# x + alpha * fx on one core: other cut points for the loads, and a last load that belongs to x

## The chip, the core and the metric

The kernel runs on one core of one Trainium2 chip. The metric is the device time of one execution in microseconds (us); lower is better. A profiled execution also has a span, from the first to the last instruction that the profiler records; the device time is a little longer than the span.

## What is computed

The reference is one line:

```python
def reference(x, fx, alpha):
    return x + alpha * fx
```

x and fx are 512 x 32 x 640 in bf16, alpha is a single bf16 number. So 20.97 MB of x and 20.97 MB of fx are read from HBM, and 20.97 MB are written back. Each element takes one multiplication and one addition.

## The kernel before

Each tensor is laid out as 128 rows, one for each SBUF partition. A row holds 80 units of K = 1024 elements (2 KiB each), that is 160 KiB. The whole of x stays in SBUF as one tile, `x_t`, and the result is written over it. fx passes through two buffers of the tile `f_t` (tag "f", two buffers), each as wide as the widest piece.

The three lists at the top of the kernel say how rows are cut: `X` (five loads of x), `F` (eight pieces of fx) and `S` (three stores), in units. A load moves the same stretch of all 128 rows. A row's stretch is one packet, so a load is 128 packets, and each of the 16 DMA engines moves eight of them; the three stores have rows of 64, 64 and 32 KiB. In this text a load's "row" is such a packet.

The order is written out by hand in `PLAN`, and each engine runs its own instructions in this order. The letters mean: `x i` and `f j` are loads, `c j` computes piece j, `s i` is a store, and `a` fetches alpha and spreads it over the partitions by a 1 x 128 matmul. All transfers, loads and stores alike, are issued by SyncE (SP in the profile) in `transfer` (line 79), one after the other, into one DMA queue. A computation is two VectorE (DVE) instructions: the product in place in `f_t` (line 97), then the sum into `x_t` (line 100).

What orders the work is this. Piece j of fx goes to the buffer that piece j-2 had, so SP may issue `f j` only when the sum of piece j-2 is done. While SP waits for that, everything behind it in `PLAN` waits too. A load of x needs no buffer to come free. A computation needs its piece of fx and all loads of x that cover its stretch. A store needs the sums of its stretch, and one entry holds the first store back further:

```python
LATE = {("s", 0): ("f", 6)}
```

With it, SP issues store 0 only after load `f 6` has landed. In the kernel before, one more load, `f 7` (units 77 to 80, rows of 6144 bytes), follows `f 6` in the queue, so it is under way when store 0 is issued.

Of the kernel before, what the change touches and what calls it, by code (L numbers as in the profile page):

```python
# [1 line left out]

# [4 lines left out]

ACT = mybir.ActivationFunctionType
ALU = mybir.AluOpType
F32 = mybir.dt.float32  # L10
BF16 = mybir.dt.bfloat16

K = 1024
P = 128


X = [(0, 4), (4, 22), (22, 44), (44, 66), (66, 80)]
F = [(0, 11), (11, 22), (22, 33), (33, 44), (44, 55), (55, 66), (66, 77), (77, 80)]
S = [(0, 32), (32, 64), (64, 80)]
N = 80  # L20

PLAN = """
x 0
x 1
a
f 0
f 1
x 2
c 0
f 2  # L30
c 1
f 3
x 3
c 2
f 4
c 3
f 5
x 4
c 4
f 6  # L40
c 5
f 7
c 6
s 0
s 1
c 7
s 2
"""
LATE = {("s", 0): ("f", 6)}


@with_exitstack
def kernel(
    ctx: ExitStack,
    tc: tile.TileContext,
    x: bass.AP,
    fx: bass.AP,
    alpha: bass.AP,
    out: bass.AP,
):  # L60
    nc = tc.nc
    xv = x.flatten_outer_dims().rearrange("(p n) d -> p (n d)", p=P)
    fxv = fx.flatten_outer_dims().rearrange("(p n) d -> p (n d)", p=P)
    ov = out.flatten_outer_dims().rearrange("(p n) d -> p (n d)", p=P)
    assert xv.shape[1] == N * K

    consts = ctx.enter_context(tc.tile_pool(name="consts", bufs=1))
    psum = ctx.enter_context(tc.tile_pool(name="psum", bufs=1, space=bass.MemoryType.PSUM))
    whole = ctx.enter_context(tc.tile_pool(name="whole", bufs=1))
    fs = ctx.enter_context(tc.tile_pool(name="fs", bufs=2))  # L70
    ctx.enter_context(tc.manual_schedule())

    sync = mybir.DependencyInfo(mybir.DependencyClass.Sync, mybir.DependencyReason.DATA)
    xt = whole.tile([P, N * K], x.dtype, name="x_t")
    ft, moved = {}, {}
    done = []

    def transfer(what, out, in_):
        r = nc.sync.dma_start(out=out, in_=in_)  # L79
        if what in LATE:  # L80
            tc.add_manual_dep(r.ins, moved[LATE[what]].ins.name, sync, reason="issue late")
        moved[what] = r
        done.append(r)

    def load_x(i):
        a, b = X[i]
        transfer(("x", i), xt[:, a * K : b * K], xv[:, a * K : b * K])

    def load_f(j):
        a, b = F[j]  # L90
        ft[j] = fs.tile([P, max(e - s for s, e in F) * K], fx.dtype, tag="f", name="f_t")
        transfer(("f", j), ft[j][:, : (b - a) * K], fxv[:, a * K : b * K])

    def compute(j):
        a, b = F[j]
        term, total = ft[j][:, : (b - a) * K], xt[:, a * K : b * K]
        nc.vector.tensor_scalar(  # L97
            out=term, in0=term, scalar1=lanes["a_f"][:], scalar2=None, op0=ALU.mult
        )
        done.append(nc.vector.tensor_tensor(out=total, in0=total, in1=term, op=ALU.add))  # L100

    def store(i):
        a, b = S[i]
        transfer(("s", i), ov[:, a * K : b * K], xt[:, a * K : b * K])

    lanes = {}

    def alpha_to_lanes():
        a_1 = consts.tile([1, 1], alpha.dtype, name="a_1")
        transfer("a", a_1[:], alpha[None, :])  # L110
        ones = consts.tile([1, P], alpha.dtype, name="ones")
        nc.vector.memset(ones[:], 1.0)  # L112
        a_ps = psum.tile([P, 1], F32, name="a_ps")
        done.append(nc.tensor.matmul(a_ps[:], ones[:], a_1[:], start=True, stop=True))  # L114
        lanes["a_f"] = consts.tile([P, 1], F32, name="a_f")
        nc.vector.tensor_copy(out=lanes["a_f"][:], in_=a_ps[:])  # L116

    does = {"x": load_x, "f": load_f, "c": compute, "s": store, "a": alpha_to_lanes}
    for step in PLAN.split("\n"):
        if step:  # L120
            what, *of = step.split()
            does[what](*map(int, of))

    rest = nc.sync.nop(nofuse=True)
    for i in done[:-1]:
        tc.add_manual_dep(rest.ins, i.ins.name, sync, reason="all but the last store")


# [1 line left out]
_INS = ['x', 'fx', 'alpha']  # L130
_OUTS = [((512, 32, 640), 'bfloat16')]


# [23 lines left out]
```

## Time and profile before

| what | value |
|---|---|
| median of 3 runs | 151.76 us (151.74 to 151.78) |
| the profiled execution's own time | 151.64 us |
| its span | 149.9 us |
| DVE busy | 67.0 us, 45% of the span, 18 instructions |
| PE, POOL busy | 0.2 us each |
| bytes moved by DMA | 62.92 MB in 2306 packets, one queue |
| time that the packets took | 97.9% of what 16 DMA engines have in the span |
| mean rate | 420 GB/s over the span |

The difference between the profiled execution's time and its span, 1.74 us, lies before the first and behind the last recorded instruction. The profiled execution is 0.12 us below the median of the runs.

The profile gives, for each DMA, the time of its issue on SP and the times at which its 16 shares landed (one for each DMA engine). The trace also has a record of each packet: its start, its duration and its size. It doesn't name the DMA engine of a packet.

### The profile page before, as it was taken

What the parts mean: (1) busy time and instruction counts of PE and PEld (TensorE: products, weight loads), DVE (VectorE), ACT (ScalarE), POOL (GpSimd) and SP (SyncE); (2) the same over time, 40 slices, a digit from 0 to 9 for tenths busy, and PEclk for the clock granted to TensorE, in tenths of its full rate; (3) what the DMA queues carried; (4) which work ended last, traced back from release to release, by engine and by line L of the source; (5) the groups of instructions that cost most, each with busy time, mean ns of one, the idle gap of its engine ahead of it and who ended that gap; (6) DMA issues with size and microseconds to landing.
All of it is one profiled execution on the core that took longest, in us unless ns stands there. A gap on an engine that the chain in (4) does not pass through costs nothing.

```text
span 149.9 us, 95 instructions
## 1 busy us (share of the span) xinstructions
PE 0.2 (0%) x1; PEld 0.1 (0%) x1; DVE 67.0 (45%) x18; POOL 0.2 (0%) x4
## 2 busy tenths in 40 slices
PE   0000000000000000000000000000000000000000
PEld 0000000000000000000000000000000000000000
DVE  0000008999900799991059999379940000000000
POOL 0000000000000000000000000000000000000000
DMA  5999899989989998898999999999796969989993
GB/s 171 473 423 472 385 439 427 481 385 505 457 349 421 433 529 385 385 481 385 433 433 423 452 421 430 409 490 525 315 542 297 560 280 560 455 385 394 429 420 157
DMA packets 2306, 62.92 MB, mean 420 GB/s; under 512 B 258, under 2 KB 258, under 8 KB 386
## 3 DMA queue, kind: packets, MB, share of 16 engines
q1 hardware_dynamic: 2306, 62.92, 97.9%
HBM read 41.94 MB, written 20.97 MB: 420 GB/s over the span
## 4 chain that ended last, share of the span: by engine, by line
DMA 46%; DVE 26%; SPq 1%; issue 0%; DVEq 0%
DMA f_t<-in_fx_dram 46%; DVE x_t L100 17%; DVE f_t L97 9%; SPq L79 1%; DVEq L97 0%
## 5 line engine op out<-in xcount | busy, mean ns | idle before, releaser
L100 DVE TENSOR_TENSOR x_t<-x_t,f_t 128x11264 bf16<-128x11264 bf16 (+1 forms) x8 | 43.9, 5492 | 0.3
L97 DVE TENSOR_SCALAR f_t<-f_t,a_f 128x11264 bf16<-128x11264 bf16 (+1 forms) x8 | 23.1, 2883 | 26.9 <-DMA f_t<-in_fx_dram 26.9
L116 DVE COPY a_f<-a_ps 128x1 f32<-128x1 f32 x1 | 0.2, 158 | 15.4 <-PE a_ps L114 15.4
L112 DVE MEMSET ones<- 1x128 bf16 x1 | 0.2, 165 | 0.8 <-PEq L141 0.8
L114 PE MATMUL a_ps<-a,ones 1*128 1x1 bf16 x1 | 0.2, 158 | 16.2 <-DMA a<-in_alpha_dram 16.2
L141 POOL MEMSET const-bfloat16-1.0<- 128x1 bf16 x1 | 0.1, 101 | 0.0
L141 POOL MEMSET const-uint8-127<- 128x1 uint8 x1 | 0.1, 101 | 0.0
L114 PEld LDWEIGHTS <-ones 1*128 1x128 bf16 x1 | 0.1, 100 | 1.0 <-DVE ones L112 1.0
L141 POOL MEMSET const-float32-0.0<- 128x1 f32 x1 | 0.1, 98 | 0.2 <-issue 0.2
L141 POOL MEMSET const-float32-1.0<- 128x1 f32 x1 | 0.1, 98 | 0.0
## 6 DMA issues: line engine op xcount, KB each, us to landing
f_t<-in_fx_dram SPq DMA_DIRECT2D x7, 2816.0 KB, 17.4
x_t<-in_x_dram SPq DMA_DIRECT2D x2, 5632.0 KB, 34.0
x_t<-in_x_dram SPq DMA_DIRECT2D x1, 4608.0 KB, 15.2
out_dram<-x_t SPq DMA_DIRECT2D x1, 4096.0 KB, 38.7
x_t<-in_x_dram SPq DMA_DIRECT2D x1, 3584.0 KB, 23.2
x_t<-in_x_dram SPq DMA_DIRECT2D x1, 1024.0 KB, 4.7
f_t<-in_fx_dram SPq DMA_DIRECT2D x1, 768.0 KB, 5.9
out_dram<-x_t SPq DMA_DIRECT2D x2, 31.1
```

The lines of the kernel that those rows point to most:

```text
L79: r = nc.sync.dma_start(out=out, in_=in_)
L97: nc.vector.tensor_scalar(out=term, in0=term, scalar1=lanes["a_f"][:], scalar2=None, op0=ALU.mult)
L100: done.append(nc.vector.tensor_tensor(out=total, in0=total, in1=term, op=ALU.add))
L112: nc.vector.memset(ones[:], 1.0)
L114: done.append(nc.tensor.matmul(a_ps[:], ones[:], a_1[:], start=True, stop=True))
L116: nc.vector.tensor_copy(out=lanes["a_f"][:], in_=a_ps[:])
L141: nc = _bacc.Bacc("TRN2", target_bir_lowering=False, num_devices=1)
```

## The change

K becomes 512, so that a unit is 1 KiB and a row has 160 of them; this alone moves no data differently. In KiB of a row, the cut points before and after are:

| | before | after |
|---|---|---|
| loads of x | 8, 36, 44, 44, 28 | 8, 38, 46, 23, 39, 6 |
| pieces of fx | 22 x 7, 6 | 23 x 6, 22 |
| stores | 64, 64, 32 | 64, 64, 32 |

The short load of 6 KiB rows, which was the last piece of fx (`f 7`), is now the last piece of x (`x 5`). It stands behind `f 6` in `PLAN` again, but its destination is a part of `x_t`, which no earlier work holds. With `f 7`, the computation `c 7` and its two DVE instructions are gone, and `c 6`, the last one now, also reads what `x 5` brings. `x 4` moves ahead of `c 3` and `f 5`. The two `f_t` buffers are 23 KiB a row where they were 22. The entry in `LATE` is the same. The bodies of the functions are not touched; their lines are one lower in number.

```diff
-K = 1024
+K = 512
 P = 128
...
-X = [(0, 4), (4, 22), (22, 44), (44, 66), (66, 80)]
-F = [(0, 11), (11, 22), (22, 33), (33, 44), (44, 55), (55, 66), (66, 77), (77, 80)]
-S = [(0, 32), (32, 64), (64, 80)]
-N = 80
+X = [(0, 8), (8, 46), (46, 92), (92, 115), (115, 154), (154, 160)]
+F = [(0, 23), (23, 46), (46, 69), (69, 92), (92, 115), (115, 138), (138, 160)]
+S = [(0, 64), (64, 128), (128, 160)]
+N = 160
...
 x 3
 c 2
 f 4
+x 4
 c 3
 f 5
-x 4
 c 4
 f 6
+x 5
 c 5
-f 7
 c 6
 s 0
 s 1
-c 7
 s 2
 """
 LATE = {("s", 0): ("f", 6)}
```

SP's order of issues is then x 0, x 1, a, f 0, f 1, x 2, f 2, f 3, x 3, f 4, x 4, f 5, f 6, x 5, s 0, s 1, s 2. Before it was x 0, x 1, a, f 0, f 1, x 2, f 2, f 3, x 3, f 4, f 5, x 4, f 6, f 7, s 0, s 1, s 2.

## The prediction

> **What bounds the kernel now.** I read the page's DMA lines first, then the queue's own waits, the timeline, the windows, and last the packet records. The page:
>
> ```profile
> span 149.9 us, 95 instructions
> PE 0.2 (0%) x1; PEld 0.1 (0%) x1; DVE 67.0 (45%) x18; POOL 0.2 (0%) x4
> q1 hardware_dynamic: 2306, 62.92, 97.9%
> DMA 46%; DVE 26%; SPq 1%; issue 0%; DVEq 0%
> ```
>
> The chain (last line) gives DVE 26%, but the 16 DMA engines are busy for 97.9% of the span: the chain follows instructions, and an instruction may wait while the queue stays full. Two windows, the loads and the stores (columns: stretch, us, busy of PE, PEld, DVE, POOL, clock, DMA share, GB/s):
>
> ```profile
> 1.70:97.50 95.80, 0.16 (x1) 0.00 (x0) 54.96 (x13) 0.00 (x0) 1.00 1.00 430
> 99.46:148.80 49.34, 0.00 (x0) 0.00 (x0) 10.87 (x4) 0.00 (x0) 1.00 0.99 427
> ```
>
> So the queue is full from the first packet (1.74 us) to the last (148.78 us). The end is set by bytes, rows, and what single engines lose. The timeline around the handover from loads to stores:
>
> ```profile
> 85.67 3.15 DVE L97 TENSOR_SCALAR f_t<-f_t,a_f 128x11264 bf16<-128x11264 bf16 x1
> 88.85 6.03 DVE L100 TENSOR_TENSOR x_t<-x_t,f_t 128x11264 bf16<-128x11264 bf16 x1
> 94.91 0.33 SPq L79 DMA_DIRECT2D f_t<-in_fx_dram  x1
> 98.45 0.82 SPq L79 DMA_DIRECT2D out_dram<-x_t  x2
> 98.46 3.15 DVE L97 TENSOR_SCALAR f_t<-f_t,a_f 128x11264 bf16<-128x11264 bf16 x1 [3.58 <-DMA f_t<-in_fx_dram]
> ```
>
> The short load f 7 is issued at 94.91, when the sum of c 5 frees its buffer, and its first row starts at 97.55: 2.64 us of notice, the least of any load but the first ones. Its rows of 6144 bytes take 236 ns at the median, but four of its 16 first rows took 638, 1287, 620 and 633 ns. No later row of it exceeds 245. Nothing like that is in the loads before it: all 896 rows of 22 KiB take 836 to 848 ns, first rows too. The one other place is the load with no notice, x 0 (issued at 0.73, first row at 1.74): rows of 309 ns whose 16 first ones take 354 to 892. The late engines stay late: the landings of the 16 shares spread over 0.44 us for f 6 (98.00 to 98.44), 0.87 for f 7 (99.93 to 100.80), 0.89 for the last store (148.22 to 149.11).
>
> **The change, part by part.**
>
> *Bytes and rows: nothing.* Rows of 22 and 44 KiB take 839 and 1665 ns at the median: 826 ns for 22 KiB, so 37.5 ns per KiB and 13 ns per row. This gives 238 for 6 KiB (measured 236) and 2416 for 64 KiB (2418). Before, the loads take 309 + 1364 + 7 x 839 + 2 x 1665 + 1065 + 236 = 12,177 ns per row set; after, x has 309 + 1440 + 1740 + 877 + 1477 + 236 and fx 6 x 877 + 839, together 12,180. Both have 13 loads. Eight rows per engine: +0.02 us. Stores are unchanged.
>
> *DVE: nothing on the path.* Seven pairs for eight. From 11264 and 3072 elements (6.03 and 1.76, 3.15 and 1.01 us) a pair costs 0.37 us at length zero, which is saved under the stores; a pair of 23 KiB takes 9.53 us from start to start, where one of 22 KiB takes 9.13 (23.15 to 32.28). The last sum ends at 110.4 both before (108.64 + 1.76) and after; store 2 is needed only when store 1's rows run out, at 138.1. Its cover is 27 us.
>
> *Does the queue run dry?* I add up the landings: f 0 lands at 23.05 + 0.60 + 0.30 = 23.95; each 23 KiB load then takes 7.01 us, 46 KiB 13.93, 39 KiB 11.82, 22 KiB 6.71. Landings: f 1 30.97, x 2 44.9, f 2 51.9, f 3 58.9, x 3 65.9, f 4 72.9, x 4 84.7, f 5 91.7, f 6 98.45, x 5 about 100.4. DVE: c 0 from 24.05, c 1 to 43.2, c 2 from 51.95 to 61.55, c 3 to 71.1, c 4 to 82.55, c 5 from 91.8 to 101.4, c 6 to 110.4. So the issues on SP: f 2 33.7, f 3 43.2, x 3 43.6, f 4 61.55, x 4 61.9, f 5 71.1, f 6 82.55, x 5 82.9. The tightest is f 4: its first row is due at 65.0 (x 3's landing less 0.9, by f 6 and f 7: 98.44 and 97.55), 3.45 us after its issue; a row follows its issue by 1.01 us (x 0), so 2.4 us are spare. Moving x 4 ahead of f 5 on SP makes it 6.6 us earlier than 68.55 and delays nobody: f 5 waits for c 3 anyway. x 5 waits for no buffer.
>
> *The handover.* Store 0 is issued when f 6 lands, 98.45, as before, with 6144-byte rows under way, as before; its first row started at 99.47 with no gap behind the front engine. Store 1 now waits for c 5's sum (101.4; before, f 7 had waited for it), with SP's queue holding only store 2 behind it; its rows are needed at 118.8. Cost nothing, cover 17 us.
>
> *The slow first rows.* This is where the change can act: x 5 is issued about 82.9, some 14.6 us ahead of its first row. If the slow rows come from the short notice, they go. What they cost: by order of time the hit engines are the first to finish f 6 (+1.05), the second or so, the eleventh and the last (+0.4 each). The third and fourth latest of the final landings are 148.68 and 148.60; the latest is 149.11. Taking the three late ones away leaves 148.60, a gain of 0.51; by the completion packets (148.78 down to 148.18) it is 0.59. If only the 1287 ns row went, 149.11 less 148.89, 0.22. Nothing would be late next: the queue only shifts. I take 0.5, near the landings. At the other bound they all stay (0), or they hit worse (below).
>
> The Trainium skill speaks against this part. Its page "DMA: Bandwidth & Descriptors", section "Latency and other measured facts", gives about 0.6 us from an HWDGE issue to the first byte; f 7's notice is four times that, so by the page the early issue gains nothing and the sum would be 151.76. The trace shows 1.01 us (x 0), also less than 2.64, yet four engines were slow; so the row alone does not settle it.
>
> **Rivals.**
>
> 1. *The notice was short (forecast).* For: only f 7 among the later loads has less than 3 us, and only it and x 0 have slow first rows; the next shortest, f 6 (issued 85.78, started 90.8, 5 us), has none. The times of three runs lie within 0.04 us, so this is no chance event of one run. Against: 12 of 16 engines were not slow with the same notice. Time: 151.76 + 0.02 - 0.5 = 151.28; with some of f 4's first rows slow, up to 151.45. In the profiled execution: span 149.4, time 151.16.
>
> 2. *The slow first rows belong to the short rows behind long ones.* For: f 7 is also the only load of 6144-byte rows; less than 0.25 us of work per row covers less of a read's delay. Against: rows two to eight are as short and not slow. x 5 has the same rows in the same place, so nothing changes: 151.78, span 149.9; 151.5 (only the 1287 ns row gone) to 151.95.
>
> 3. *Slow first rows on the wrong engine (slower).* The place is the first row of x 5, or of f 4 with its 3.45 us. Before, the row of +1.05 us fell on the engine that was first done, 0.43 us ahead of the last (97.55 against 97.98), and so cost the end some 0.6. On the last engine all of it counts: +1.05 in place of +0.6, 0.45 later than now, 152.2; with a second such set at f 4 as well (+0.4) 152.6. It decides (0.3 us, 0.2%) once a first row on the rearmost engine exceeds its usual time by over 0.9 us. For: nothing seen ties the long row to the front engine. Against: three of the four were only +0.4.
>
> 4. *The change doesn't do what it says.* x 5 could be held on SP by f 6's wait for c 4 (82.55); even at c 5's end, 101.4, its first row would start at 102.4 and the queue be dry from 98.0, 4.4 us, about 156. By the order of issues that wait isn't there. I give it no chance of its own.
>
> **How the numbers follow.** This kernel's measurement tells about 0.2%, 0.3 us, from no change. Chances: case 1, a gain over 0.3, 0.46; case 2, with the weaker gain of 0.22 us that is inside 0.2%, 0.29; case 3 0.25. So faster 0.46, same 0.29, slower 0.25. The likeliest is 151.28; its own range is 151.1 (gain 0.6 and a little) to 151.45. The range of all reaches from 151.1 over case 2 up to 152.2, the nearer part of case 3; what lies above is put at 0.13, below 151.1 at 0.05.
>
> **What would show it.** Right: x 5 issued near 83, sixteen first rows of about 236 ns, landings of the last load and of the last store within 0.5 us of each other, a span near 149.4, the DMA share over 98%. Case 2: slow first rows at x 5 and the old spread of 0.9. Case 3: a spread over 1.2 us. The working on the queue is wrong if any DMA engine idles between 60 and 70 us, or the windows before 97.5 fall below a share of 0.99. The forecast is wrong outright if rows of 23 or 39 KiB take more than 37.5 ns per KiB.

## The result, and the profile after

The changed kernel takes 151.34 us (median of 22 runs, 151.17 to 151.51); the kernel before, run beside it, 151.84 (22 runs, 151.13 to 152.42). The ratio is 0.9967, with a 95% interval from 0.9957 to 0.9977: a gain of 0.50 us, or 0.33%. A second comparison gave 151.31 against 151.66, ratio 0.9976 (0.9965 to 0.9986). The profiled execution took 151.26 us with a span of 149.5, where 151.64 and 149.9 were measured before. Not only the median moved: the runs of the kernel before spread over 1.29 us, those of the changed kernel over 0.34, and the best runs of both lie within 0.04 us of each other (151.13 and 151.17).

The page of the changed kernel, its lines on the span, the engines, the DMA queue and the chain:

```profile
span 149.5 us, 93 instructions
PE 0.2 (0%) x1; PEld 0.1 (0%) x1; DVE 66.7 (45%) x16; POOL 0.2 (0%) x4
q1 hardware_dynamic: 2306, 62.92, 98.2%
DMA 41%; DVE 31%; issue 1%; SPq 1%; DVEq 0%
```

Packets and bytes are the same, and the share of the 16 DMA engines went from 97.9% to 98.2%: the same work in a shorter span. The two long windows of the changed kernel (columns as in the prediction: stretch, us, busy of PE, PEld, DVE, POOL, clock, DMA share, GB/s):

```profile
1.70:97.50 95.80, 0.16 (x1) 0.00 (x0) 53.44 (x13) 0.00 (x0) 1.00 1.01 430
99.46:148.80 49.34, 0.00 (x0) 0.00 (x0) 11.14 (x3) 0.00 (x0) 1.00 0.99 427
```

The rates are those of before, 430 and 427 GB/s. So nothing was gained in the long stretches of loads or stores. The timeline around the handover, changed kernel:

```profile
83.08 0.42 SPq L78 DMA_DIRECT2D x_t<-in_x_dram  x1
91.90 3.29 DVE L96 TENSOR_SCALAR f_t<-f_t,a_f 128x11776 bf16<-128x11776 bf16 x1 [9.23 <-DMA f_t<-in_fx_dram]
95.22 6.29 DVE L99 TENSOR_TENSOR x_t<-x_t,f_t 128x11776 bf16<-128x11776 bf16 x1
98.59 12.40 SPq L78 DMA_DIRECT2D out_dram<-x_t  x3
101.43 3.15 DVE L96 TENSOR_SCALAR f_t<-f_t,a_f 128x11264 bf16<-128x11264 bf16 x1
```

The short load, now x 5, is issued at 83.08, 14.6 us ahead of its first row at 97.71. All 128 rows of it take 234 to 246 ns; before, four first rows took 620 to 1287. From here on, a row is called slow when it took over 60 ns longer than the median of its load. Its landings spread over 0.40 us (100.05 to 100.45), as those of f 6 do (0.42), and not over 0.87.

A window shows the late engines directly. It begins at 100.20 us, when an engine that lost nothing has already started its first row of store 0, and ends before any engine starts the second. What starts in it comes from engines that are behind. The kernel before:

```profile
100.20:101.80 1.60, 0.00 (x0) 0.00 (x0) 1.56 (x2) 0.00 (x0) 1.00 0.20 86
```

The changed kernel:

```profile
100.20:101.80 1.60, 0.00 (x0) 0.00 (x0) 1.60 (x2) 0.00 (x0) 1.00 0.00 0
```

86 GB/s over 1.6 us is 0.138 MB: two rows of 64 KiB and one of 6 KiB, started by the two latest engines. After the change nothing starts there. A late engine has the same rows of all stores still to move, and the last one ends the kernel: the final landings run from 148.22 to 149.11 before, and from 148.37 to 148.73 after.

### The profile page after: what moved, and what is told of

Its sections match the earlier page's. It is cut to its first block, busy times and chain, and to the rows that moved or that the text cites. A ratio compares the mean times of both kernels' runs of the same rounds, so it can differ in the third digit from the quotient of the medians.

```text
span 149.5 us, 93 instructions
## 1 busy us (share of the span) xinstructions
PE 0.2 (0%) x1; PEld 0.1 (0%) x1; DVE 66.7 (45%) x16; POOL 0.2 (0%) x4
## 3 DMA queue, kind: packets, MB, share of 16 engines
q1 hardware_dynamic: 2306, 62.92, 98.2%
## 4 chain that ended last, share of the span: by engine, by line
DMA 41%; DVE 31%; issue 1%; SPq 1%; DVEq 0%
DMA f_t<-in_fx_dram 41%; DVE x_t L99 20%; DVE f_t L96 11%; SPq L78 1%; DVEq L96 0%
## 5 line engine op out<-in xcount | busy, mean ns | idle before, releaser
L99 DVE TENSOR_TENSOR x_t<-x_t,f_t 128x11776 bf16<-128x11776 bf16 (+1 forms) x7 | 43.8, 6254 | 0.2
L96 DVE TENSOR_SCALAR f_t<-f_t,a_f 128x11776 bf16<-128x11776 bf16 (+1 forms) x7 | 22.9, 3265 | 26.7 <-DMA f_t<-in_fx_dram 26.7
```

The source lines that it names most:

```text
L96: nc.vector.tensor_scalar(out=term, in0=term, scalar1=lanes["a_f"][:], scalar2=None, op0=ALU.mult)
```

## The experiments

The theory: a load that is issued too short a time ahead of its first row has slow first rows on some DMA engines, and the latest engine carries that to the end. The rivals: the new cut points, the new destination in `x_t`, or the short rows of 6144 bytes themselves. "Notice" is the time from a load's issue on SP to the start of its first row on the engine that starts first.

**The yardstick.** The changed kernel again.

> The changed kernel once more, as the yardstick for the others of this call. Both theories: about 0.9967 of the kernel before (some 151.3 us), x 5 issued near 83 us, its sixteen first rows all between 230 and 250 ns, the landings of the last load within 0.45 us of each other.

151.31 us, ratio 0.9976 (0.9965 to 0.9986); x 5's rows 234 to 245 ns; no slow row. The spread of the last load's landings was 0.58, not below 0.45, but so it was for every load from x 0 on (0.60): this profile's engines lost it in the first load.

**The short notice put back, all else kept.** Two lines of the plan change places, and x 5 waits for the product of c 5 (cuts are marked by three dots here and below):

```diff
+c 5
 x 5
-c 5
...
-LATE = {("s", 0): ("f", 6)}
+LATE = {("s", 0): ("f", 6), ("x", 5): ("product", 5)}
...
-        nc.vector.tensor_scalar(
+        r = nc.vector.tensor_scalar(
...
+        moved[("product", j)] = r
```

> The changed kernel with one wait added: x 5 is issued only after the product of c 5, at about 95.1 us, which leaves its first row (due at 97.7) some 2.6 us of notice, as f 7 had. Sizes, destination and order on the queue stay as in the changed kernel. Theory of the short notice: some of x 5's first rows take 400 to 1300 ns again, the landings spread to 0.6 to 1.0 us, and the time goes back by 0.3 to 0.6 us, to a ratio of 0.998 to 1.001. Rival (the gain came from the new cut points or from the destination that no earlier work holds): first rows stay near 236 ns and the ratio stays 0.9967.

152.33 us (151.84 to 152.75), ratio 1.0041 (1.0025 to 1.0057). That is 1.0 us above the yardstick, more than expected, and slower than the kernel before. The timeline of this kernel and the same window as above:

```profile
95.24 0.33 SPq L78 DMA_DIRECT2D x_t<-in_x_dram  x1
```

```profile
100.20:101.80 1.60, 0.00 (x0) 0.00 (x0) 1.60 (x2) 0.00 (x0) 1.00 0.34 146
```

The notice came out as 2.41 us (first row at 97.65), 0.23 shorter than f 7's. Six rows of x 5 took 347 to 1208 ns, and its landings spread over 1.38 us. The cut points and the destination were those of the fast kernel, so neither protects by itself.

**Less notice, and something in between.** In the next two kernels c 5's sum or product is cut in two instructions, and x 5 waits for the first one. The edit against the changed kernel, for the sum (in the plan, x 5 stands behind c 5 as above):

```diff
-LATE = {("s", 0): ("f", 6)}
+LATE = {("s", 0): ("f", 6), ("x", 5): ("sum", 5)}
...
+        for s in [slice(0, 1408), slice(1408, None)] if (j, "sum") == (5, 'sum') else [slice(0, None)]:
+            r = nc.vector.tensor_tensor(
+                out=total[:, s], in0=total[:, s], in1=term[:, s], op=ALU.add
+            )
+            moved.setdefault(("sum", j), r)
+            done.append(r)
```

> As the kernel with x 5 behind the product of c 5, but x 5 waits until the first 1408 columns of c 5's sum are done, at about 96.1 us: 1.6 us of notice, where x 0 shows 1.0 us from issue to first row. Theory of the short notice: more of the sixteen first rows are slow than with 2.6 us (8 to 16 of them), the spread of the landings goes to 0.8 to 1.3 us, the time 0.5 to 1.0 us above the changed kernel, ratio 1.000 to 1.004. Rival: no slow rows as long as the queue isn't dry, ratio 0.9967.

153.52 us (152.86 to 154.12), ratio 1.0115 (1.0089 to 1.0141): 2.2 us above the yardstick, twice the most that was expected. The issue came at 96.31, 1.25 us ahead of the first row at 97.56. Eighteen rows were slow, later rows of x 5 among them, and its landings spread over 2.68 us.

With the product cut at 6144 columns:

> Between the changed kernel and the one with x 5 behind the product of c 5: x 5 is issued when the first 6144 columns of that product are done, near 93.8 us, some 3.9 us ahead of its first row. The runs so far give no slow row with 5 us or more, one of sixteen now and then with 3.5 (f 4), four to six with 2.5. Theory of the short notice, as a matter of degree: none to two slow first rows, time 0 to 0.3 us above the changed kernel's 151.31. Rival that any wait on a VectorE instruction just ahead costs the microsecond, whatever the notice: about 152.3 again.

151.27 us (151.19 to 151.42), ratio 0.9969 (0.9958 to 0.9980). x 5 was issued at 93.65, 3.96 us ahead; no row was slow and the spread was 0.42. A wait on VectorE just ahead costs nothing, then; the time that it leaves does.

**Short notice for long rows.** f 4, rows of 23 KiB behind rows of 23 KiB, waits for the first 2880 columns of c 3's product, which is cut in two instructions for that; x 5 stays early.

```diff
+c 3
 f 4
 x 4
-c 3
...
-LATE = {("s", 0): ("f", 6)}
+LATE = {("s", 0): ("f", 6), ("f", 4): ("product", 3)}
...
```

> The changed kernel with f 4, a load of 23 KiB rows behind 23 KiB rows, held until the first 2880 columns of c 3's product are done, at about 62.6 us: 2.6 us of notice for a first row that is due near 65.2. x 5 stays early. Theory of the short notice: first rows of f 4 are slow by 0.1 to 1 us on some engines, the spread of its landings grows from 0.39 us to 0.5 to 0.9 and stays so to the end, time 0.1 to 0.5 us above the changed kernel, ratio 0.997 to 1.000. Rival that slow first rows belong to short rows behind long ones: nothing at f 4, ratio 0.9967.

152.37 us (151.71 to 152.91), ratio 1.0046 (1.0028 to 1.0064). Notice 2.60 us (62.64 to 65.24). Four first rows of f 4 took 1378 to 1775 ns in place of 876, and its landings spread over 0.95 us in place of 0.41. The window in which an undisturbed engine has begun x 4 already, first for this kernel, then for the changed one:

```profile
72.65:73.30 0.65, 0.00 (x0) 0.00 (x0) 0.00 (x0) 0.00 (x0) 1.00 0.57 246
```

```profile
72.65:73.30 0.65, 0.00 (x0) 0.00 (x0) 0.24 (x1) 0.00 (x0) 1.00 0.00 0
```

So the slow first rows do not belong to short rows behind long ones. The time went up by 1.1 us, twice the most that was expected; in the profiled execution (151.90 us), a quieter one of this kernel, the final landings end 0.63 us later than in the changed one.

The expectation also said that the spread stays to the end, and it does not: it is 1.00 us for x 5, 0.55 for store 0 and 0.45 for the last store. The engines that lost nothing had to wait. By `LATE`, store 0 is issued when the last share of f 6 has landed, and here that share came late, so the issue moved from 98.59 to 99.24. Twelve engines were done with x 5 between 99.62 and 100.02 and began store 0 only between 100.08 and 100.23. The window in which the changed kernel has begun store 0 on most engines, first for the kernel with f 4 held, then for the changed one:

```profile
99.40:99.90 0.50, 0.00 (x0) 0.00 (x0) 0.50 (x1) 0.00 (x0) 1.00 0.69 283
```

```profile
99.40:99.90 0.50, 0.00 (x0) 0.00 (x0) 0.50 (x1) 0.00 (x0) 1.00 4.19 1794
```

So a spread that gets smaller need not be a loss made good: here the others were held back to the slowest.

**A time or a number of rows.** f 4 stands behind rows of 40 KiB, and is issued behind the first 2176 columns of c 3's sum, which is cut in two for that. In the plan, c 3 stands ahead of f 4, as in the run just told.

```diff
-X = [(0, 8), (8, 46), (46, 92), (92, 115), (115, 154), (154, 160)]
+X = [(0, 8), (8, 46), (46, 92), (92, 132), (132, 154), (154, 160)]
...
-LATE = {("s", 0): ("f", 6)}
+LATE = {("s", 0): ("f", 6), ("f", 4): ("sum", 3)}
...
```

> How far ahead must a load be issued: a time, or a number of rows? f 4 stands behind rows of 40 KiB (1516 ns each, x cut at 8, 38, 46, 40, 22, 6) and is issued when the first 2176 columns of c 3's sum are done, near 66.3 us, some 3.9 us ahead of its first row at 70.2. That is as much time as x 5 had with 6144 columns of the product (3.96 us, 4.7 rows of 839 ns, no slow row), but only 2.6 rows ahead, fewer than the 3.0 to 3.1 rows of the cases with slow first rows. If it is a time: no slow rows beyond a single one, 151.3 us. If it is a number of rows: four or more slow first rows at f 4, 151.8 to 152.6 us.

151.31 us (151.24 to 151.42), ratio 0.9975 (0.9962 to 0.9987). Issued at 66.18, 4.06 us or 2.7 rows of 1516 ns ahead, no row of f 4 was slow. It is a time and not a number of rows, as far as this one run against the others tells. The bytes queued ahead are not told apart from the time: 4.06 us were 2.7 rows of 40 KiB and 3.96 us 4.7 rows of 22 KiB, both some 105 KiB on each engine.

**The kernel before with an early f 7, its cut points and its kind of destination kept.** f 7 goes to the first 6 KiB of the buffer that it had, and c 5's sum frees those first.

```diff
-        ft[j] = fs.tile([P, max(e - s for s, e in F) * K], fx.dtype, tag="f", name="f_t")
+        if j == 7:
+            ft[j] = ft[5]
+        else:
+            ft[j] = fs.tile([P, max(e - s for s, e in F) * K], fx.dtype, tag="f", name="f_t")
...
-        done.append(nc.vector.tensor_tensor(out=total, in0=total, in1=term, op=ALU.add))
+        for s in [slice(0, 3 * K), slice(3 * K, None)] if j == 5 else [slice(0, None)]:
+            done.append(
+                nc.vector.tensor_tensor(
+                    out=total[:, s], in0=total[:, s], in1=term[:, s], op=ALU.add
+                )
+            )
```

> The kernel before, all its cut points kept, with one thing changed: f 7 goes to the first 6 KiB of the buffer that it had, and the sum of c 5 is two instructions, of 3072 and 8192 columns, so that f 7 need wait for the first only. It is issued near 90.6 us in place of 94.91, some 6.9 us ahead of its first row. Theory of the short notice: no slow first rows, the spread of f 7's landings some 0.45 us, the time of the changed kernel (151.2 to 151.4 us) and its narrow spread over the runs. Rival, that the cut points or the destination in x brought part of the gain: it stays above 151.5, or its runs spread over 0.8 us as those of the kernel before do.

151.30 us (151.21 to 151.41), ratio 0.9969 (0.9957 to 0.9981): the whole gain, and the narrow spread. The timeline of f 7's issue and the window of the late engines:

```profile
90.92 0.33 SPq L79 DMA_DIRECT2D f_t<-in_fx_dram  x1
```

```profile
100.20:101.80 1.60, 0.00 (x0) 0.00 (x0) 1.60 (x1) 0.00 (x0) 1.00 0.00 0
```

6.8 us of notice, no slow row of f 7, landings within 0.49 us. But for c 5's sum in two instructions, the issue 4 us earlier is all that is different from the kernel before, and it brings what the change brought.

**The last load as fx, issued early.** x in five loads; the last two pieces of fx, 16 and 6 KiB, share one buffer.

```diff
-X = [(0, 8), (8, 46), (46, 92), (92, 115), (115, 154), (154, 160)]
-F = [(0, 23), (23, 46), (46, 69), (69, 92), (92, 115), (115, 138), (138, 160)]
+X = [(0, 8), (8, 46), (46, 92), (92, 115), (115, 160)]
+F = [(0, 23), (23, 46), (46, 69), (69, 92), (92, 115), (115, 138), (138, 154), (154, 160)]
...
-x 5
+f 7
 c 5
 c 6
 s 0
 s 1
+c 7
...
+        if j == 7:
+            ft[j] = ft[6][:, 16 * K :]
...
```

> The last short load is the end of fx again (rows of 6144 bytes), as in the kernel before, but it shares one buffer with the piece of 16 KiB before it, so that it can be issued right behind that, near 83 us. x is loaded in five pieces. Theory of the short notice: as fast as the changed kernel within 0.1 us, no slow first rows. Rival that it takes a destination in x, which no earlier work holds: slow first rows and some 151.7 to 152.

151.33 us (151.20 to 151.50), ratio 0.9974 (0.9962 to 0.9985), f 7 issued at 83.21 and no slow row in it. A place in x isn't needed, only an early issue.

**Three tries for more.** More notice for f 4, by the same cut points as in the kernel with 40 KiB rows:

> A candidate for a better version: the changed kernel with x cut at 8, 38, 46, 40, 22, 6 KiB in place of 8, 38, 46, 23, 39, 6. The load ahead of f 4 is 17 KiB a row longer, which gives f 4 some 8.6 us of notice in place of 3.5, and all else its place. Theory of the short notice: the odd slow first row at f 4 is gone, time 0 to 0.1 us below the changed kernel. Rival: nothing to gain, the same time.

151.31 us (151.16 to 151.37), ratio 0.9976 (0.9963 to 0.9988): no gain that can be told. f 4 had none, but now f 6 was issued at 87.88, 3.1 us ahead, and had one first row of 992 ns in place of 839.

Store 0 without its wait, `LATE = {}`:

> The changed kernel without the entry in LATE: store 0 is issued right behind x 5, near 83.5 us, and not when f 6 has landed. By the queue's order nothing moves, since store 0's rows start only behind x 5's: the same 151.3 us within 0.1. Rival: the short notice of store 0 (1 us) costs it something too, and the early issue brings 0.1 to 0.5 us. Second rival: rows of a store queued behind loads hold something up, and it is slower by 0.2 us or more.

151.50 us (151.38 to 151.88), ratio 0.9990 (0.9976 to 1.0003), 0.2 us above the 151.31 of the changed kernel. Windows over the last rows of x 5, this kernel first:

```profile
98.40:99.40 1.00, 0.00 (x0) 0.00 (x0) 1.00 (x1) 0.00 (x0) 1.00 1.05 344
```

```profile
98.40:99.40 1.00, 0.00 (x0) 0.00 (x0) 1.00 (x1) 0.00 (x0) 1.00 0.99 412
```

With store 0's rows queued behind them, 25 of the later rows of x 5 took 305 to 592 ns in place of 236: 344 GB/s for 412. So the entry in `LATE` earns 0.2 us, and the second rival was right, just: it had said 0.2 us or more. What in the queue slows these rows was not tried.

One first load of x, rows of 46 KiB in place of 8 and 38:

> A candidate for a faster version. The first load of all has no notice either: in the changed kernel the 128 rows of x 0 (8 KiB, 309 ns each undisturbed) take 10.5 us too long together, 0.65 us per engine. Here x 0 and x 1 are one load of 46 KiB rows, so that each engine has one row without notice, and one row set less (13 ns times 8 is 0.1 us). If the loss is one cold start per engine, of up to 0.6 us, whatever the row: 151.2 to 151.3, nothing but the row set. If it falls on several short rows of each engine because they are short: 150.9 to 151.1. Slower, if the load of 46 KiB rows starts later than one of 8 KiB.

151.57 us (151.47 to 151.72), ratio 0.9991 (0.9980 to 1.0003): worse by some 0.26. The sixteen first rows took 1909 to 3152 ns in place of 1740, together 11.6 us too long (0.73 per engine; x 0's rows lost 0.51 to 0.71 per engine over the profiles), and the landings of the loads stayed 0.77 us apart. The loss of the start isn't a matter of many short rows, and the short first load is the better one.

All cases by notice, times above the changed kernel's 151.31. The kernel before took 151.66 to 151.84 beside the several runs, so a difference of 0.1 us between rows tells nothing:

| load | notice, us | slow rows in the profile | spread of its landings, us | time, us |
|---|---|---|---|---|
| x 5, behind part of c 5's sum | 1.25 | 18 | 2.68 | +2.2 |
| x 5, behind c 5's product | 2.41 | 6 | 1.38 | +1.0 |
| f 4, held | 2.60 | 7, 4 of them by 0.5 to 0.9 us | 0.95 | +1.1 |
| f 7 of the kernel before | 2.64 | 4 | 0.87 | +0.35 to +0.5 |
| f 6, with x 3 of 40 KiB rows | 3.1 | 1, by 0.15 to 0.22 us | 0.43 to 0.49 | 0 |
| f 4 of the changed kernel, two profiles | 3.25 and 3.49 | none, and 1 by 0.08 us | 0.57 and 0.41, as in the load before | 0 (itself) |
| x 5, behind part of the product | 3.96 | 0 | 0.42 | 0 |
| f 7 in the kernel before, early | 6.8 | 0 | 0.49 | 0 |

In six more of these kernels f 4 has 3.1 to 3.5 us of notice too: three of them show no slow row in it, three show one, by 0.17 to 0.22 us. So between 3 and 3.5 us a single slow row still comes now and then.

## Why the prediction was right

*The forecast mechanism held.* The short notice was the cause, by both directions: taking it from the changed kernel brought the slow rows back, giving it to the kernel before brought the whole gain, with the cut points and the kind of destination kept. The forecast of 151.28 is 0.06 from the measured 151.34.

*Bytes and rows.* Right: 23 KiB rows take 876 ns (877 was worked out), 38 KiB 1439 (1440), 46 KiB 1740 (1740), 39 KiB 1479 (1477).

*The queue's sum.* f 6 landed at 98.58 (98.45 forecast), x 5 at 100.45 (100.4), f 4 was issued at 61.68 (61.55), x 5 at 83.08 (82.9), store 1 at 101.54 (101.4). The common 0.13 was there after x 0, whose rows lost 0.15 us more per engine in this execution. The queue did not run dry.

*The size of the gain.* The 0.5 us came from single engines of one profile. In the profiles the final landing moved by 0.38 (149.11 to 148.73); with the start that was later by 0.13 taken off it is 0.51. The medians moved by 0.50 in one comparison and 0.35 in the other.

*What was wrong in the reasoning.* The argument that three runs within 0.04 us exclude chance failed. Over 22 runs the kernel before spreads from 151.13 to 152.42, and 19 of them lie above the slowest run of the changed kernel (151.51). So the slow rows seem to be there in most executions, on other engines or by other amounts each time; one execution alone has a profile, so this is read from the times and not seen. So 0.5 was a good size by luck of the profile as much as by the working. Nor is it quite so that the loads ahead of f 7 show nothing like it, x 0 apart: seven rows of x 1, issued 3.49 us ahead, took 1398 to 1487 ns where 1364 is the median, two of them first rows. They left the spread of the landings as it was (0.46 and 0.45 us). And 12 engines of 16 without a slow row, held against the theory, are what a notice at the edge looks like: at 1.25 us far more rows are slow, at 3.96 none.

*Rival 3 was priced about right, at another place.* A time of 152.2 to 152.6 did not come from the changed kernel, but 0.23 us less notice than f 7 had gives 152.33, and 2.6 us at f 4 gives 152.37. f 4's notice, which it named (3.45 us by its sum, 3.25 and 3.49 measured), was just enough: one first row of 956 ns for 876, in one of the two profiles of the changed kernel. The way to the end was another one at f 4 than rival 3 had it: the late engine also held back store 0 on twelve others.

*The rule weighed.* The 0.6 us from issue to first byte that the Trainium skill states ("DMA: Bandwidth & Descriptors", "Latency and other measured facts") would, read alone, have let 2.64 us be ample. The runs decide otherwise: 2.4 to 2.6 us cost 0.35 to 1.1 us here, behind a full queue, and from about 3 us on nothing measurable was lost.

## What to carry to other kernels

Where a full DMA queue sets the end, "the queue never runs dry" isn't enough: look at the first rows of each load and at the spread of its 16 landings. Where the spread grows, look at how long before its first row that load was issued. Look too at what waits for the last share of a load, as store 0 does here: such a wait can hold the other engines back to the latest. Here some 4 us between issue and first row were safe and 2.6 were not, and the cure can be small: free the needed part of a buffer first, or give the load a place that nobody holds. Judge such an effect over many runs, since three may happen to agree.

## What the runs showed of the hardware that was not expected

- The cost rises as notice falls, for x 5 from nothing at 3.96 us to +1.0 at 2.41 and +2.2 at 1.25, though the queue had rows to move all the while and a first row can start 1.01 us after its issue (x 0). Notice alone doesn't set the cost: f 4 at 2.60 cost +1.1 and f 7 at 2.64 at most half of that, and what makes the difference was not tried. What the slow rows wait for inside the DMA engines, the trace doesn't show, and it stays open.
- A loss on one DMA engine isn't made good by the others: 0.87 us of spread at f 7 was still 0.89 at the end, 48 us later. Where the spread shrank at the handover (1.00 to 0.55 us with f 4 held), twelve engines had stood idle ahead of store 0.
- Short notice cost the loads, not store 0: where it is held back it starts 0.84 to 1.01 us after its issue, and none of its rows took over 2468 ns, with a median of 2418 to 2420.
- A store queued behind a short load made the load's later rows slower (305 to 592 ns in place of 236), 0.2 us in all.
